# Sliding-window attention and an ELU feed-forward in one kernel: w_in loaded as fp32 and cast on chip, v loaded and shifted by key block, part of ELU on ACT

## The chip, the cores and the metric

The kernel runs on one core of one Trainium2 chip. The metric is device time in microseconds (us). Engines are named as in the profile: PE (TensorE), DVE (VectorE), ACT (ScalarE), POOL (GpSimd), SP (SyncE). Transfers are issued by SP, ACT and POOL, each into its own queue of the same 16 DMA engines: q1 is SP's, q10 ACT's, q0 POOL's.

## The reference

q, k and v have shape 8 x 8 x 576 x 64 (batch, heads, sequence, head size), w_in is 512 x 2048, w_out is 2048 x 512, all fp32.

```python
scores = scale * np.matmul(q, k.transpose(0, 1, 3, 2))        # scale = 1/8
mask = np.abs(pos[:, None] - pos[None, :]) <= 32
scores = np.where(mask, scores, -1e9)
attn = softmax(scores)
x = (attn @ v).transpose(0, 2, 1, 3).reshape(4608, 512)
h = x @ w_in
g = np.where(h > 0.0, h, np.exp(np.minimum(h, 0.0)) - 1.0)
out = g @ w_out
```

## The kernel before

**Attention.** A batch has nine query blocks of 64 rows; two blocks that follow each other make a pair i, and there are 36 pairs. q and k are loaded as fp32 in halves of four heads (`L`, into `stg`), cast to bf16 (`C`, into `bf`), transposed on PE (`T`) and evicted from PSUM (`E`, into `qT` and `kT`). For a pair, `QK` makes the scores of 64 queries against a window of 128 keys, `SM` takes exp on ACT, `MK` multiplies by the band's mask on DVE, `AV` multiplies by v for four heads at a time (g = 0 and 1), with a column of ones that gives the row sum, and `RN` divides. `X` brings the 128 x 512 result into the layout that the feed-forward needs: pairs 0 to 3 over PE and PSUM (`XT`, then a copy `XE`), the others by a DMA transpose from SP.

**v by key block.** `vw` holds v of a batch as nine windows of 128 keys that overlap by half. The even windows are loaded from memory (`LV`, five transfers from POOL that cast to bf16 on the way). The odd windows are made of halves of their even neighbours by two copies from SBUF to SBUF (`SV`, on SP). There are three `vw` buffers.

**Feed-forward.** Tokens go in tiles of 2, 2, then eight times 4 pairs. For each of the 16 column blocks fo of w_in, `H` computes h in PSUM, `EX` takes exp on ACT, `FF` makes f = min(exp(h) - 1, 0) and `GG` makes g = max(h, f), both on DVE. `Y` multiplies by w_out in four parts of four fo each; `YC` evicts and `OUT` stores. w_in and w_out are loaded and cast by POOL's transfers, four each (`WI`, `WO`). `g` has two buffers and `psH`, the PSUM tiles of h, three.

**Order.** Nothing is scheduled by the engines. `Plan` takes every step with an engine, an assumed duration, a rank and its predecessors, replays them in a list schedule, and emits each engine's instructions in the order that comes out. An engine then executes strictly in that order. A step with `at` is assumed to be done no sooner than that; a step with `dma` goes through an assumed transfer server. These assumed times only set the order. The order of the transfers of batches 0 and 1 and of the weights is thereby set on each of SP, ACT and POOL.

The ELU steps in the kernel before:

```python
nc.vector.tensor_scalar(f, e, -1.0, 0.0, ALU.add, ALU.min)      # FF
nc.vector.tensor_tensor(gs[t][:, fo, :], ps, f, ALU.max)        # GG
```

Of the kernel before, what the change touches and what calls it, by code (L numbers as in the profile page):

```python
# [8 lines left out]
FP32 = mybir.dt.float32  # L9
BF16 = mybir.dt.bfloat16  # L10
AX = mybir.ActivationFunctionType
ALU = mybir.AluOpType
# [8 lines left out]
class Plan:  # L21
# [15 lines left out]
    def run(self):  # L37
        ops = self.ops
        done, users, left = {}, {}, {}
        for n, o in ops.items():  # L40
            left[n] = len(o[3])
            for d in o[3]:
                assert d in ops, (n, d)
                users.setdefault(d, []).append(n)
        free = {}
        server = 2.0
        ready = {}
        for n, o in ops.items():
            free.setdefault(o[0], 0.0)
            if left[n] == 0:  # L50
                ready.setdefault(o[0], {})[n] = 0.0
        order = []
        while len(order) < len(ops):
            best = None
            for e, rs in ready.items():
                if not rs:
                    continue
                t = max(free[e], min(rs.values()))
                n = min((ops[n][2], n) for n, r in rs.items() if r <= t)[1]
                if best is None or t < best[0]:  # L60
                    best = (t, e, n)
            t, e, n = best
            del ready[e][n]
            _, dur, _, _, fn, dma, lag, at = ops[n]
            free[e] = t + dur
            if dma:
                server = max(server, t + dur) + dma
                end = server + 2.0
# [20 lines left out]
def kernel(  # L89
# [9 lines left out]
    nc = tc.nc  # L99

    B, H, S, D = q.shape
    WIN = 32
# [4 lines left out]
    QB = 64  # L107
    NQB = S // QB
# [86 lines left out]
            nc.vector.tensor_copy(dst, src)  # L195


    def load_v(b):
        vt = vw[b % NVB]
        vb = v[b].rearrange("h s d -> s h d")  # L200
        nc.gpsimd.dma_start(out=vt[WIN:128, 0, :, 0:D], in_=vb[0:128 - WIN])
        for qb in range(2, NQB - 1, 2):
            lo = qb * QB - WIN
            nc.gpsimd.dma_start(out=vt[:, qb, :, 0:D], in_=vb[lo:lo + 128])  # L204
        lo = (NQB - 1) * QB - WIN
        nc.gpsimd.dma_start(out=vt[0:S - lo, NQB - 1, :, 0:D], in_=vb[lo:S])  # L206

    def shift_v(b):
        vt = vw[b % NVB]
        nc.sync.dma_start(out=vt[0:QB, 1:NQB:2], in_=vt[QB:128, 0:NQB - 1:2])  # L210
        nc.sync.dma_start(out=vt[QB:128, 1:NQB:2], in_=vt[0:QB, 2:NQB:2])


    def QK(i):
# [73 lines left out]

    def XE(i):
        dst, pt = live.pop(("XT", i))  # L290
        nc.vector.tensor_copy(dst, pt)


    gs, es, ys = {}, {}, {}
# [12 lines left out]
    def EX(t, fo):  # L307
# [2 lines left out]
        nc.scalar.activation(e, ps, AX.Exp)  # L310
        es[t, fo] = (ps, e)

    def FF(t, fo):
        ps, e = es[t, fo]
        f = ep.tile([128, ps.shape[1]], BF16, name="f", tag="f")
        nc.vector.tensor_scalar(f, e, -1.0, 0.0, ALU.add, ALU.min)  # L316
        es[t, fo] = (ps, f)

    def GG(t, fo):
        ps, f = es.pop((t, fo))  # L320
        nc.vector.tensor_tensor(gs[t][:, fo, :], ps, f, ALU.max)  # L321

    def ypool(t, c):
        if t < NT - 1:
# [54 lines left out]
    def prank(i):  # L379
# [6 lines left out]
    LAND = {(0, "k", 0): 6.2, (0, "q", 0): 8.2, (0, "k", 1): 10.5,  # L386
            (0, "q", 1): 13.0, (1, "k", 0): 27.0, (1, "q", 0): 31.0,
            (1, "k", 1): 35.0, (1, "q", 1): 39.0}
    for b in range(B):
        need = prank(b * NQB // 2)  # L390
        r0 = need - 60
        t0 = where[b * NQB // 2][0]
        early = [("H", max(t0 - 2, 0), 15 if t0 == 2 else 8)] if b > 1 else []
        for half in range(2):
            for nm in ("q", "k"):
                deps = list(early)
                if b == 1:
                    deps.append(("SM", 0))
                if b:
                    deps.append(("C", b - 1, nm, half))  # L400
                P.op(("L", b, nm, half), "ACT" if b else "SP", 0.1,
                     r0 + half, deps,
                     lambda b=b, nm=nm, half=half: load_qk(
                         b, nm, half, nc.scalar if b else nc.sync),
                     dma=0.0 if b < 2 else 2.2, lag=2.0,
                     at=LAND.get((b, nm, half), 0.0))
                eng = casts0[nm, half] if b == 0 else "POOL"
                deps = [("L", b, nm, half)]
                if b >= 2:
                    deps += [("T", b - 2, nm, hp) for hp in range(HP)]  # L410
                P.op(("C", b, nm, half), eng, cdur[eng], need - 30 + half, deps,
                     lambda b=b, nm=nm, half=half, eng=eng:
                     cast(b, nm, half, engs[eng]))
        deps = list(early)
        if b > 1:
            deps += [("WO", c) for c in range(NWC)]
        if b >= NVB:
            last = ((b - NVB + 1) * NQB - 1) // 2
# [3 lines left out]
        P.op(("LV", b), "POOL", 4.5, (-2000, -899)[b] if b < 2 else r0, deps, lambda b=b: load_v(b),  # L422
             dma=5.0 if b > 1 else 0.0, at=(17.0, 45.0)[b] if b < 2 else 0.0)
        P.op(("SV", b), "SP", 0.2, need - 20, [("LV", b)],
             lambda b=b: shift_v(b), lag=4.5)
        for hp in range(HP):
            for nm in ("q", "k"):
                n = hp * 2 + (nm == "k")
                deps = [("C", b, nm, hp // 2)]
                m = n - (4 if b == 0 else 1)  # L430
                if m >= 0:
                    deps.append(("E", b, "qk"[m % 2], m // 2))
                elif b:
                    deps.append(("E", b - 1, "k", HP - 1))
                P.op(("T", b, nm, hp), "PE", 0.3, need - 36 + 4 * n, deps,
                     lambda b=b, nm=nm, hp=hp: T(b, nm, hp))
                deps = [("T", b, nm, hp)]
                if b >= NKB:
                    last = ((b - NKB + 1) * NQB - 1) // 2
                    deps.append(("QK", last))  # L440
                P.op(("E", b, nm, hp), EVAC[nm, hp], 0.7, need - 36 + 4 * n, deps,
                     lambda b=b, nm=nm, hp=hp: E(b, nm, hp))

    for c in range(NWC):
        P.op(("WI", c), "POOL", 1.0, -990 + c,
             [("C", 0, "k", 1)], lambda c=c: WI(c),
             at=(19.5, 24.0, 28.5, 33.0)[c])
        P.op(("WO", c), "POOL", 1.0, -890 + c, [("C", 1, "q", 1)],
             lambda c=c: WO(c),
             at=(50.0, 54.0, 58.0, 62.0)[c])  # L450

    for i in range(NPAIR):
        r = prank(i)
# [13 lines left out]
        P.op(("MK", i), "DVE", 0.85, r, deps, lambda i=i: MK(i))  # L467
        t, c = where[i]
        for g in range(2):
            deps = [("MK", i)] + [("SV", b) for b in bs]  # L470
            if i < NC0:
                if i:
                    deps.append(("RN", i - 1, g))
# [14 lines left out]
        if i < NC0:  # L488
            if i:
                deps.append(("X", i - 1))  # L490
            P.op(("XT", i), "PE", 0.3, r + 3, deps, lambda i=i: X(i))
            P.op(("X", i), "DVE", 0.42, r + 3, [("XT", i)],
                 lambda i=i: XE(i))
        else:
            P.op(("X", i), "SP", 1.2, r + 3, deps, lambda i=i: X(i), lag=4.0)

    hseq = [(t, fo) for t in range(NT) for fo in range(NFO)]
    for n, (t, fo) in enumerate(hseq):
        np_ = tiles[t][1]
        fr = np_ / 4  # L500
        r = PER * tiles[t][0] + 2 * fo * fr
        deps = [("X", tiles[t][0] + np_ - 1), ("WI", fo * NWC // NFO)]
        if n >= 3:
            deps.append(("GG",) + hseq[n - 3])
        if t >= 2:
# [8 lines left out]
        P.op(("FF", t, fo), "DVE", 0.1 + 0.33 * fr, r, [("EX", t, fo)],  # L514
             lambda t=t, fo=fo: FF(t, fo))
        P.op(("GG", t, fo), "DVE", 0.16 + 0.53 * fr, r, [("FF", t, fo)],
             lambda t=t, fo=fo: GG(t, fo))
# [83 lines left out]
```

The softmax here doesn't subtract the row's maximum and nothing guards it: scores larger than these inputs give would overflow.

## Time and profile before

| what | value |
|---|---|
| median of 3 runs | 367.59 us (363.65 to 368.04) |
| the profiled execution | 366.73 us, its span 364.8 us |
| PE busy | 314.2 us (86%) |
| DVE busy | 252.9 us (69%) |
| ACT busy | 177.2 us (49%) |
| POOL busy | 86.1 us (24%) |
| transfers | 46.13 MB, mean 126 GB/s |

The page gives busy time of each engine, its share in 40 equal slices, the DMA queues, a chain of work followed back from the last instruction, groups of instructions by source line, and transfer issues. Times in the trace's answers are counted from the start of the span. A group's line names the source line, the engine, the operation and the tiles written and read. Matmul ends are modelled, so a busy PE need not be at its peak. The idle time of an engine is named after what ended it.

### The profile page before, as it was taken

The page shows a single profiled execution, that of the slowest core. Times are in us where ns is not written, and L with a number is a line of the kernel's source. Part 1 is how long each engine was busy: PE and PEld are TensorE (multiplying, and loading weights), DVE is VectorE, ACT ScalarE, POOL GpSimd, SP SyncE. Part 2 cuts the span into 40 slices and gives each one's busy share as a digit, 9 for nine tenths or more (in the row PEclk, how much of TensorE's full clock was granted, in tenths as well). Part 3 has the DMA queues.
Part 4 walks back from the last instruction along what each step waited for, and adds up shares of the span by engine and source line. Part 5 has one row for each costly group of instructions (what it writes and reads, how often), then busy time and mean ns, then how long its engine had stood idle before and what let it go on. Part 6 is the DMA issues. An engine that isn't in the chain of part 4 may idle for free.

```text
span 364.8 us, 7010 instructions
## 1 busy us (share of the span) xinstructions
PE 314.2 (86%) x2725; PEld 168.9 (46%) x2768; DVE 252.9 (69%) x565; ACT 177.2 (49%) x290; POOL 86.1 (24%) x93
## 2 busy tenths in 40 slices
PE   1415889669877999999999999989999999999995
PEld 1314666334434544554455445445554444444442
DVE  4216899475779499886887787778788778756610
ACT  3431477236453654754565466555654535443421
POOL 7623810490036004500540240033000000000000
PEclk9999999899999899999999999999999999999999
DMA  8999999999698639994995793195112121111012
GB/s 173 172 251 276 121 198 194 196 135 174 147 242 102 72 101 214 131 138 105 242 127 69 175 210 85 45 234 114 45 51 66 46 58 45 43 49 40 29 65 78
DMA packets 81504, 46.13 MB, mean 126 GB/s; under 512 B 56384, under 2 KB 76864, under 8 KB 81472
## 3 DMA queue, kind: packets, MB, share of 16 engines
q0 software_dynamic: 41728, 8.92, 33.4%
q1 hardware_dynamic: 28544, 20.26, 25.4%
q10 hardware_dynamic: 11200, 16.52, 19.0%
q8 instruction: 21, 0.34, 0.4%
q14 instruction: 11, 0.09, 0.1%
HBM read 36.70 MB, written 9.44 MB: 126 GB/s over the span
## 4 chain that ended last, share of the span: by engine, by line
PE 58%; DVE 18%; DMA 14%; issue 3%; ACTq 2%; POOL 2%; ACT 1%; SPq 1%; POOLq 0%; DVEq 0%
PE psY L335 24%; PE psH L302 24%; DMA vw<-vw 6%; DVE g L321 6%; DVE f L316 6%; DMA xt<-xs 5%; DVE pm L243 4%; PE psO L255 4%; DMA vw<-in_v_dram 3%; PE psT L180 2%; DVE xs L270 2%; ACTq L155 2%; PE psS L220 2%; PE psO L335 1%; PE psS L335 1%
## 5 line engine op out<-in xcount | busy, mean ns | idle before, releaser
L302 PE MATMUL psH<-xt,w_in_sb 128*128 128x512 bf16 (+1 forms) x624 | 147.3, 360 | 4.5 <-DVE g L321 2.4
L310 ACT ACTIVATE e<-psH 128x512 f32<-128x512 f32 (+1 forms) x160 | 88.1, 555 | 115.9 <-PE psH L302 90.1
L335 PE MATMUL psY<-w_out_sb,g 128*128 128x512 bf16 x501 | 131.8, 383 | 3.1 <-ACT y L341 1.1
L316 DVE TENSOR_SCALAR f<-e 128x512 bf16<-128x512 f32 (+1 forms) x160 | 75.7, 473 | 45.8 <-ACT e L310 45.7
L321 DVE TENSOR_TENSOR g<-psH,f 128x512 bf16<-128x512 f32 (+1 forms) x160 | 102.0, 637 | 5.1
L302 PEld LDWEIGHTS <-w_in_sb 128*128 128x128 bf16 x640 | 60.4, 99 | 61.2 <-issue 6.1
L335 PEld LDWEIGHTS <-g 128*128 128x128 bf16 x576 | 52.3, 98 | 55.0 <-issue 2.7
L170 POOL CAST bf<-stg 96x1536 bf16<-96x1536 f32 x29 | 43.5, 1501 | 107.1 <-DMA stg<-in_k_dram 89.1
L255 PE MATMUL psO<-vw,pm 128*128 128x65 bf16 x544 | 30.7, 198 | 17.9 <-DMA vw<-vw 8.3
L231 ACT ACTIVATE pu<-psS 128x1024 bf16<-128x1024 f32 x36 | 36.8, 1021 | 12.7 <-PE psS L220 10.3
L255 PEld LDWEIGHTS <-pm 128*128 128x128 bf16 x576 | 27.1, 102 | 30.9 <-issue 8.1
L243 DVE TENSOR_TENSOR pm<-pu,masks 128x512 bf16<-128x512 bf16 x72 | 34.0, 514 | 4.8 <-ACT pu L231 4.8
L180 PEld LDWEIGHTS <-bf 96*128 96x128 bf16 x384 | 23.7, 104 | 28.2 <-ACT bf L168 8.1
L270 DVE TENSOR_TENSOR xs<-psO,rc 128x256 bf16<-128x256 f32 x68 | 28.9, 424 | 5.5 <-DMA xt<-xs 3.2
L180 PE MATMUL psT<-ident,bf 96*128 96x96 bf16 x348 | 25.4, 211 | 7.0 <-POOL bf L170 3.6
L341 ACT COPY y<-psY 128x512 f32<-128x512 f32 x33 | 19.4, 586 | 19.4 <-PE psY L335 14.3
L268 DVE RECIPROCAL rc<-psO 128x4 f32<-128x4 f32 x68 | 12.1, 178 | 22.0 <-PE psO L255 21.5
L193 ACT COPY qT<-psT 128x576 bf16<-128x576 bf16 x30 | 19.1, 638 | 15.9 <-PE psT L180 15.9
L204 POOL DMA_DIRECT2D vw<-in_v_dram x24 | 21.3, 900 | 15.5 <-PE psO L255 15.3
L220 PE MATMUL psS<-qT,kT 64*128 64x64 bf16 x576 | 16.0, 196 | 3.6 <-ACT pu L231 3.2
L220 PEld LDWEIGHTS <-kT 64*128 64x128 bf16 x576 | 11.3, 98 | 15.3 <-issue 14.5
L206 POOL DMA_DIRECT2D vw<-in_v_dram x8 | 6.5, 812 | 41.4 <-PE psO L255 40.6
(42 smaller groups left out, 74.1 us busy)
## 6 DMA issues: line engine op xcount, KB each, us to landing
out_dram<-y SPq DMA_DIRECT2D x36, 256.0 KB, 2.1
stg<-in_k_dram ACTq DMA_DIRECT2D x14, 576.0 KB, 9.3
stg<-in_q_dram ACTq DMA_DIRECT2D x14, 576.0 KB, 10.9
vw<-vw SPq DMA_DIRECT2D x16, 260.0 KB, 8.5
vw<-in_v_dram POOLq DMA_DIRECT2D x24, 128.0 KB, 8.2
w_in_sb<-in_moe_w_in_dram POOLq DMA_DIRECT2D x4, 512.0 KB, 13.7
w_out_sb<-in_moe_w_out_dram POOLq DMA_DIRECT2D x4, 512.0 KB, 11.3
vw<-in_v_dram POOLq DMA_DIRECT2D x16, 96.0 KB, 11.4
```

What stands on the lines that cost most here:

```text
L170: eng.tensor_copy(dst, src)
L180: nc.tensor.transpose(pt[:, j, :], src[:, j, 2 * hp:2 * hp + 2, :], ident[0:PR, 0:PR])
L220: nc.tensor.matmul(psS[:, h % 2, s, hp, :], lhsT=kT[b % NKB][base:base + 64, hp, qb * QB:qb * QB + 128], rhs=qT[b % NKB][base:base + 64, h ...
L231: nc.scalar.activation(pu, live.pop(("S", i)), AX.Exp, scale=SCALE)
L243: nc.vector.tensor_mul(dst, pu[:, :, s], mb)
L255: nc.tensor.matmul(o[:, j, :], lhsT=p[:, h, s * QB:s * QB + 128], rhs=vw[b % NVB][:, qb, h, :], start=(s == 0), stop=(s == 1))
L270: nc.vector.tensor_mul(live["X", i][:, g * HP:(g + 1) * HP, :], o[:, :, 0:D], rb)
L302: nc.tensor.matmul(ps, lhsT=w_in_sb[:, do, fo * 128:(fo + 1) * 128], rhs=xts[t][:, do, :], start=(do == 0), stop=(do == NDO - 1))
L310: nc.scalar.activation(e, ps, AX.Exp)
L316: nc.vector.tensor_scalar(f, e, -1.0, 0.0, ALU.add, ALU.min)
L321: nc.vector.tensor_tensor(gs[t][:, fo, :], ps, f, ALU.max)
L335: nc.tensor.matmul(ps, lhsT=gs[t][:, fo, c * 128:(c + 1) * 128], rhs=w_out_sb[:, fo, :], start=(fo == 0), stop=(fo == NFO - 1))
```

## The change

- w_in: four transfers `WL` on SP bring it as fp32 into buffers of the `g` pool. Eight casts `WI` (four chunks, two halves each) on POOL and ACT write `w_in_sb`.
- v: `LV` is a step for each even window, and `SV` for batches 0 and 1 is split in two, the first odd window and the other three. `AV` names as its predecessors only the windows that it reads.
- ELU: in tiles 0 and 1, for odd fo, f' = relu(1 - exp(h)) is made on ACT, and g = max(-f', h) on DVE.
- The copy `XE` of pairs 0 to 3 is on ACT.
- The predecessors, ranks and assumed landing times of the loads of batches 0 to 2 and of w_out are changed with it, and with them the order of the instructions.

```diff
-    def load_v(b):
+    def load_v(b, qb):
         vt = vw[b % NVB]
         vb = v[b].rearrange("h s d -> s h d")
...
+        lo, hi = max(0, qb * QB - WIN), min(S, qb * QB - WIN + 128)
+        r = lo - (qb * QB - WIN)
+        nc.gpsimd.dma_start(out=vt[r:r + hi - lo, qb, :, 0:D], in_=vb[lo:hi])
+
+    def shift_v(b, w0, w1):
         vt = vw[b % NVB]
...
+        nc.sync.dma_start(out=vt[0:QB, w0:w1 - 1:2],
+                          in_=vt[QB:128, w0 - 1:w1 - 1:2])
+        nc.sync.dma_start(out=vt[QB:128, w0:w1 - 1:2],
+                          in_=vt[0:QB, w0 + 1:w1:2])
...
     def XE(i):
         dst, pt = live.pop(("XT", i))
-        nc.vector.tensor_copy(dst, pt)
+        nc.scalar.copy(dst, pt)
...
+    def fact(t, fo):
+        return t < 2 and fo % 2 == 1
...
+        if fact(t, fo):
+            nc.scalar.activation(f, e, AX.Relu, bias=1.0, scale=-1.0)
+        else:
+            nc.vector.tensor_scalar(f, e, -1.0, 0.0, ALU.add, ALU.min)
...
+        if fact(t, fo):
+            nc.vector.scalar_tensor_tensor(gs[t][:, fo, :], f, -1.0, ps,
+                                           ALU.mult, ALU.max)
+        else:
+            nc.vector.tensor_tensor(gs[t][:, fo, :], ps, f, ALU.max)
...
-    def WI(c):
-        nc.gpsimd.dma_start(out=w_in_sb[:, :, c * FC:(c + 1) * FC],
-                            in_=w_in_v[:, :, c * FC:(c + 1) * FC])
+    wst = {}
+
+    def WL(c):
+        n = c // 2
+        if n not in wst:
+            wst[n] = gp.tile([128, 2, NDO, FC], FP32, name="g", tag="g")
+        nc.sync.dma_start(out=wst[n][:, c % 2],
+                          in_=w_in_v[:, :, c * FC:(c + 1) * FC])
+
+    def WI(c, half):
+        src = wst[c // 2][:, c % 2, 2 * half:2 * half + 2, :]
+        dst = w_in_sb[:, 2 * half:2 * half + 2, c * FC:(c + 1) * FC]
+        if WENG[half] == "ACT":
+            nc.scalar.copy(dst, src)
+        else:
+            engs[WENG[half]].tensor_copy(dst, src)
...
+    WENG = ("POOL", "ACT")
...
-        early = [("H", max(t0 - 2, 0), 15 if t0 == 2 else 8)] if b > 1 else []
+        early = [("H", max(t0 - 2, 0), 2 if b == 2 else 8)] if b > 1 else []
...
                 if b == 1:
-                    deps.append(("SM", 0))
+                    deps.append(("WI", 1, 1))
...
         if b == 1:
-            deps.append(("C", 0, "k", 1))
...
+            deps.append(("WI", 2, 0))
+        for qb in range(0, NQB, 2):
+            P.op(("LV", b, qb), "POOL", 0.9,
...
+        groups = [(1, 3), (3, 9)] if b < 2 else [(1, 9)]
+        for w0, w1 in groups:
+            P.op(("SV", b, w0), "SP", 1.2, need - 20 + 0.1 * w0,
+                 [("LV", b, x) for x in range(w0 - 1, w1, 2)],
+                 lambda b=b, w0=w0, w1=w1: shift_v(b, w0, w1), lag=4.5)
...
+        P.op(("WL", c), "SP", 0.5, -990 + c, [("L", 0, "q", 1)],
+             lambda c=c: WL(c), at=(16.0, 20.0, 24.0, 28.0)[c])
...
-        P.op(("WO", c), "POOL", 1.0, -890 + c, [("C", 1, "q", 1)],
+        P.op(("WO", c), "POOL", 1.0, -890 + c, [("WI", NWC - 1, 0)],
...
+                if qb % 2 == 0:
+                    deps.append(("LV", b, qb))
+                else:
+                    deps += [("SV", b, w0) for w0, w1 in SVOF[b]
+                             if w0 <= qb < w1]
```

More of the change, by code (lines that the diff above doesn't have):

```diff
@@ L67, in run @@
                 server = max(server, t + dur) + dma
-                end = server + 2.0
+                end = server + 2.0 + lag
             else:
@@ L195, in E @@
             nc.vector.tensor_copy(dst, src)
-    def load_v(b):
+    def load_v(b, qb):
         vt = vw[b % NVB]
         vb = v[b].rearrange("h s d -> s h d")
[L201 to L208, printed above, removed]
+        lo, hi = max(0, qb * QB - WIN), min(S, qb * QB - WIN + 128)
+        r = lo - (qb * QB - WIN)
+        nc.gpsimd.dma_start(out=vt[r:r + hi - lo, qb, :, 0:D], in_=vb[lo:hi])
+    def shift_v(b, w0, w1):
         vt = vw[b % NVB]
-        nc.sync.dma_start(out=vt[0:QB, 1:NQB:2], in_=vt[QB:128, 0:NQB - 1:2])
-        nc.sync.dma_start(out=vt[QB:128, 1:NQB:2], in_=vt[0:QB, 2:NQB:2])
+        nc.sync.dma_start(out=vt[0:QB, w0:w1 - 1:2],
+                          in_=vt[QB:128, w0 - 1:w1 - 1:2])
+        nc.sync.dma_start(out=vt[QB:128, w0:w1 - 1:2],
+                          in_=vt[0:QB, w0 + 1:w1:2])
     def QK(i):
@@ L315, in FF @@
         f = ep.tile([128, ps.shape[1]], BF16, name="f", tag="f")
-        nc.vector.tensor_scalar(f, e, -1.0, 0.0, ALU.add, ALU.min)
+        if fact(t, fo):
+            nc.scalar.activation(f, e, AX.Relu, bias=1.0, scale=-1.0)
+        else:
+            nc.vector.tensor_scalar(f, e, -1.0, 0.0, ALU.add, ALU.min)
         es[t, fo] = (ps, f)
@@ L320, in GG @@
         ps, f = es.pop((t, fo))
-        nc.vector.tensor_tensor(gs[t][:, fo, :], ps, f, ALU.max)
+        if fact(t, fo):
[3 more added lines that the diff above has]
+            nc.vector.tensor_tensor(gs[t][:, fo, :], ps, f, ALU.max)
     def ypool(t, c):
@@ L385 @@
     cdur = {"DVE": 1.2, "ACT": 1.5, "POOL": 1.5}
-    LAND = {(0, "k", 0): 6.2, (0, "q", 0): 8.2, (0, "k", 1): 10.5,
-            (0, "q", 1): 13.0, (1, "k", 0): 27.0, (1, "q", 0): 31.0,
-            (1, "k", 1): 35.0, (1, "q", 1): 39.0}
+    LAND = {(0, "k", 0): 6.2, (0, "q", 0): 7.7, (0, "k", 1): 9.2,
+            (0, "q", 1): 11.0, (1, "k", 0): 30.0, (1, "q", 0): 33.0,
+            (1, "k", 1): 36.0, (1, "q", 1): 39.0}
+    SVOF = {}
+    WENG = ("POOL", "ACT")
     for b in range(B):
@@ L404 @@
                          b, nm, half, nc.scalar if b else nc.sync),
-                     dma=0.0 if b < 2 else 2.2, lag=2.0,
+                     dma=0.0 if b < 2 else 2.2,
+                     lag=2.0 if b < 2 else 5.0,
                      at=LAND.get((b, nm, half), 0.0))
@@ L420 @@
         if b == 1:
-            deps.append(("C", 0, "k", 1))
[L422 to L425, printed above, removed]
+            deps.append(("WI", 2, 0))
+        for qb in range(0, NQB, 2):
+            P.op(("LV", b, qb), "POOL", 0.9,
+                 (-999, -899)[b] + 0.1 * qb if b < 2 else r0 + 0.1 * qb,
+                 deps, lambda b=b, qb=qb: load_v(b, qb),
+                 dma=1.0 if b > 1 else 0.0, lag=2.0,
+                 at=(13.0, 41.0)[b] + 0.6 * qb if b < 2 else 0.0)
+        groups = [(1, 3), (3, 9)] if b < 2 else [(1, 9)]
[3 more added lines that the diff above has]
+                 lambda b=b, w0=w0, w1=w1: shift_v(b, w0, w1), lag=4.5)
+        SVOF[b] = groups
         for hp in range(HP):
@@ L444 @@
     for c in range(NWC):
-        P.op(("WI", c), "POOL", 1.0, -990 + c,
-             [("C", 0, "k", 1)], lambda c=c: WI(c),
-             at=(19.5, 24.0, 28.5, 33.0)[c])
-        P.op(("WO", c), "POOL", 1.0, -890 + c, [("C", 1, "q", 1)],
+        P.op(("WL", c), "SP", 0.5, -990 + c, [("L", 0, "q", 1)],
+             lambda c=c: WL(c), at=(16.0, 20.0, 24.0, 28.0)[c])
+        for half in range(2):
+            P.op(("WI", c, half), WENG[half],
+                 {"ACT": 0.95, "POOL": 1.05, "DVE": 0.7}[WENG[half]],
+                 -980 + c, [("WL", c)],
+                 lambda c=c, half=half: WI(c, half))
+        P.op(("WO", c), "POOL", 1.0, -890 + c, [("WI", NWC - 1, 0)],
              lambda c=c: WO(c),
-             at=(50.0, 54.0, 58.0, 62.0)[c])
+             at=(46.0, 50.0, 54.0, 58.0)[c])
     for i in range(NPAIR):
@@ L469 @@
         for g in range(2):
-            deps = [("MK", i)] + [("SV", b) for b in bs]
+            deps = [("MK", i)]
+            for x in (2 * i, 2 * i + 1):
+                b, qb = divmod(x, NQB)
+                if qb % 2 == 0:
[3 more added lines that the diff above has]
+                             if w0 <= qb < w1]
             if i < NC0:
@@ L491 @@
             P.op(("XT", i), "PE", 0.3, r + 3, deps, lambda i=i: X(i))
-            P.op(("X", i), "DVE", 0.42, r + 3, [("XT", i)],
+            P.op(("X", i), "ACT", 0.42, r + 3, [("XT", i)],
                  lambda i=i: XE(i))
@@ L501 @@
         r = PER * tiles[t][0] + 2 * fo * fr
-        deps = [("X", tiles[t][0] + np_ - 1), ("WI", fo * NWC // NFO)]
+        deps = [("X", tiles[t][0] + np_ - 1), ("WI", fo * NWC // NFO, 0),
+            ("WI", fo * NWC // NFO, 1)]
         if n >= 3:
@@ L513 @@
              lambda t=t, fo=fo: EX(t, fo))
-        P.op(("FF", t, fo), "DVE", 0.1 + 0.33 * fr, r, [("EX", t, fo)],
+        P.op(("FF", t, fo), "ACT" if fact(t, fo) else "DVE",
+             0.1 + 0.33 * fr, r, [("EX", t, fo)],
              lambda t=t, fo=fo: FF(t, fo))
```

## The prediction

> **What bounds the kernel now.** I read the page's row of slices first, then the chain of waits, then busy time by stretch, and last the DMA queues in windows of 2 us.
>
> ```profile
> span 364.8 us, 7010 instructions
> PE   1415889669877999999999999989999999999995
> DVE  4216899475779499886887787778788778756610
> DMA  8999999999698639994995793195112121111012
> ```
>
> A slice is 9.1 us. From the 14th slice on (120 us) PE stands at nine tenths or more. Before that it idles some 40 us in all, and in the same slices the DMA engines are full. The end is therefore moved by whatever moves the first 90 us.
>
> ```profile
> 36.00:48.00 12.00, 10.26 (x99) 7.67 (x98) 10.51 (x33) 6.50 (x16) 9.27 (x10) 1.00 1.98 122
> 48.00:60.00 12.00, 11.12 (x149) 8.11 (x149) 10.90 (x34) 8.65 (x19) 0.00 (x0) 1.00 1.53 208
> 200.00:250.00 50.00, 47.77 (x412) 24.57 (x418) 39.80 (x83) 27.16 (x44) 12.01 (x9) 1.00 0.74 157
> ```
>
> The columns are the stretch, its length, then PE, weight loads, DVE, ACT and POOL busy. Tiles 0 and 1 (36 to 60 us) have DVE at 21.4 of 24 us; later stretches are PE's.
>
> ```profile
> 7.39 11.70 DMA vw<-in_v_dram
> 19.10 10.88 DMA vw<-vw
> 36.12 1.86 PE psH L302 x8
> 60.58 13.35 DMA xt<-xs
> ```
>
> From the chain (start, length): v of batch 0 loads, then the shift of its blocks (SV.0) lands at 30.0, then AV runs, and the first H matmul starts at 36.1. So the gate of the whole kernel is one SBUF copy of 512 packets that lands late in a full DMA system. Why it is late is in the queues (packets, MB, share of 16 engines), here for 4:6, 10:12, 14:16, 18:20 and 34:36 us:
>
> ```profile
> q1 hardware_dynamic: 290, 0.43, 110.0%
> ...
> q1 hardware_dynamic: 286, 0.43, 102.5%
> q0 software_dynamic: 167, 0.02, 16.5%
> ...
> q0 software_dynamic: 2229, 0.28, 359.4%
> ...
> q0 software_dynamic: 399, 0.40, 123.9%
> ...
> q10 hardware_dynamic: 323, 0.48, 82.0%
> q0 software_dynamic: 330, 0.08, 40.9%
> ```
>
> q1 is SP's queue, q10 ACT's, q0 POOL's. POOL issues v at 3.9, yet q0 moves nothing until about 10.5, while q1 runs at 145 packets per us. Alone, v's small packets run at 1,100 per us; beside a queue with work they get one turn for each turn of the other (323 against 330), whatever their size. The w_in load alone makes 200 packets per us.
>
> **What the Trainium skill says.** "DMA: Bandwidth & Descriptors", section "Queues, rings and completion order", says that each DMA engine takes turns between the queue rows it has work for, and that a ring is consumed in order. The trace agrees: 323 against 330, and the four q/k loads on q1 land one after the other (5.7 to 12.3 us after issue). The same page, "SWDGE vs HWDGE vs iDMA", says that only GpSimd's DMAs can cast, so fp32 loads from SP need casts on engines. "ScalarE: Activation LUTs", section "Table sets: the hidden batching unit", says relu is in every table set, so exp and relu need no switch; the trace has one table load (1.28 us at 0.80), but no relu.
>
> **The change, part by part.**
>
> *w_in on SP (WL).* Four loads of 512 packets of 2 KB now follow the q/k loads on q1 at about 2.8 us, with no wait. On the order of the changed program SP then issues SV.0 behind them, so in q1's ring the shifts cannot start before w_in has passed. q1 has sent 1,181 packets by 10 us and the last of the 1,536 q/k packets passes at about 12.7. For w_in beside v: a 2 KB packet takes 99 ns (123.9% x 32 us / 399) and a v packet about 33; the full windows overlap by a factor 1.2 (82.0 + 40.9%), so a pair costs 110 ns on each of 16 engines, 145 pairs per us. Bounds: 200 per us (w_in alone) and 120 (w_out's pace beside SV.1 at 50 us). I take 145: w_in passes at 12.7 + 14.1 = 26.8 us (22.9 to 29.8).
>
> *v of batch 0.* Turn by turn with q1 it gets only 290 + 2,048 = 2,340 of its 4,608 packets by then; before it had all at 17.1. The first small shift (128 packets) passes by 27.7 and lands at about 29.2. So pair 0 gains a microsecond at most, although its own v blocks are in by 25.
>
> *The loads of batch 1 (L.1).* They now stand on ACT behind WI.1.1: SM.0, the cast WI.0.1 (1.0 us; the 96x1536 cast took 1.47), SM.1, SM.2, WI.1.1 end at about 24.0. Before, 3.5 us passed from issue to first packet, so q10 wakes at 27.5, just when q1 is done. Three of the four loads (1,152 packets at 160 per us, 7.2 us) then hold v to their pace: v has 2,470 + 1,150 at 34.9, the last 990 take 0.9, and v lands at about 37.0. If w_in is as fast as its bound, v is through at 25 and lands at 26; if q10 wakes 2 us later, at 31.
>
> *The second shift (SV.0.3).* It needs the last v block. Two issues of 0.6, 384 packets at 116 per us (SV beside v, 84 to 86 us) 3.3, 0.7 to the first packet, 1.2 to land: 42.8 against 30.0 before. Pair 1 needs it, and H.0.0 needs pair 1. In the changed program the fourth load of L.1 waits for the semaphore that the first half of this shift raises (eight semaphores go round among the SP and ACT transfers). Behind that issue on ACT stand SM.3, XE.0, WI.2.1 and XE.1 (0.8 + 1.0 + 0.4 + 1.0 + 0.4). AV.1, its normalisation and XT.1 take about 2.4 beside them. H.0.0 starts at about 45.3, 9.2 later than at 36.1; QK.3, AV.0 and three w_in casts are then done, which is why the 12.8 shrink.
>
> *Casts of w_in on POOL.* Hidden: they wait for data, and POOL has nothing due. WO now waits on POOL for v to land (again the round of semaphores), and the casts of batch 1 stand behind it until about 48; T.1 is due behind H.0.13, at about 55. Without that cover it would cost what POOL is late.
>
> *f on ACT for half of tiles 0 and 1, XE on ACT.* DVE loses 16 x 0.29 and 4 x 0.42 = 6.3 us and keeps the g instructions: the new one reads the same PSUM operand, so I price it at the old 0.42 (0.40 to 0.55). ACT gains 16 x 0.40 (priced at e's 0.38 plus gap; 0.33 to 0.5). Its sum from EX.0.0 to EX.1.15: e 32 x 0.40 = 12.8, f 6.0, seven q/k evictions 4.6, two SM 2.1, XE 0.9, WI.3.1 1.0, L.2's issues 2.4: 29.8. DVE ran this stage at 92% before, so ACT gets 31 us. PE's work there is only 22.6.
>
> *Order of PE.* AV.4 to AV.8 and almost all of Y.0 and Y.1 move out of tile 1's H stage to a stretch of their own before H.2.0: 10 AV x 0.41, 8 T x 0.42, 4 QK x 0.41, 11 Y x 0.86 = 18.6, with hand-overs 20. L.2 is issued earlier relative to the compute, so the PE stall for its cast (66.4 to 69.5 before) goes.
>
> *Sum.* With as many H and Y groups behind it as the changed kernel has at H.2.0, the kernel before stood at 89.9 us: 53.8 after its H.0.0. Now it is 31 + 20 = 51. Total: +9.2 - 2.8 = +6.4. The same PE work is left from there on, and steady tiles are untouched. The profiled execution took 366.7 (span 364.8 and 1.9 around it), 0.9 below the median shown, so 366.7 + 6.4 = 373.1; I say 373.
>
> **The rivals.** A is the forecast: v is held to the pace of w_in and then of L.1. For it: the equal turns at 34 to 36 us. Its own range, from w_in's pace and q10's start, is 367 to 379.
>
> B: the gate opens when w_in is through. If v is in before q10 wakes, SV.0.3 follows w_in directly and lands at 30 to 31; with the shorter way to H this gives H.0.0 at 34, and 366.7 - 2 - 2.8 = 362; if DVE's relief gives the whole 4.5 us that f was worth and PE's T stall (3.1) goes too, 357. For it: w_in alone ran at 200 per us. Against: w_in is not alone, and v starts at 10.5 only.
>
> C, the slower side: ACT as the bound of tiles 0 and 1. Place: EX, f and the evictions in one in-order queue, where an eviction of batch 1 waits for PE's T and everything behind it waits too. 29.8 us of work at 80% instead of 96% is 37 us, +6 on the forecast: 379. It decides from about 33 us on, where the total passes 375. For it: ACT waited 90 us in all for H before and its f now joins that loop. Against: f waits on its own engine's e, which saves one hand-over.
>
> **How the numbers follow.** A 0.48, B 0.20, C 0.32. Two per cent, 7.3 us, is about what a measurement of this kernel can tell from no change: under 360.2 and over 375. A gives 0.32 within and 0.16 slower, B 0.11 faster and 0.09 within, C 0.05 within and 0.27 slower: faster 0.11, same 0.46, slower 0.43. The range 361 to 382 leaves out B's best and C's worst.
>
> **What would show it.** Right: q0 and q1 with equal counts from 11 to 27 us; v's last packets at 35 or later; the first AV near 29 and the second a dozen microseconds after it; H.0.0 at 43 to 47; ACT over nine tenths in the two slices after. Wrong: H.0.0 before 38, q0 at over 300 packets per us beside w_in, or steady tiles that differ.

## The result, and the profile after

The changed kernel takes 380.1 us (median of 4 runs, 378.8 to 382.1) against 367.6 before: ratio 1.036, 95% interval 1.028 to 1.044, slower. Forecast were 373.0 us and a range of 361 to 382. The profiled execution took 378.8 us, with a span of 377.1 (364.8 before). The ratios in this document leave disturbed executions out, so a median shown beside one can lie higher than the ratio says.

The page's rows of slices, after (a slice is 9.4 us):

```profile
span 377.1 us, 7071 instructions
PE   1502387899697799999899989998999999999995
DVE  5211275874389777978897688669868887756510
ACT  4430377874354356465456446554765544444321
DMA  8999993999979819995997294349111221101011
```

PE has a longer hole in slices 3 to 5 (19 to 47 us: 0, 2, 3), and the DMA engines have one in their seventh slice (57 to 66 us: 3). The chain of waits up to 50 us (start, length):

```profile
7.42 27.22 DMA vw<-in_v_dram
34.66 8.78 DMA vw<-vw
46.50 1.01 PE psH L301 x4
```

The last v load of batch 0 is in the chain for 27.2 us (11.7 before), the shift of its later blocks begins at 34.7 (19.1), and H.0.0 stands at 46.5 (36.1). The queues at 14:16, 24:26 and 34:36 us (packets, MB, share of 16 engines) say why:

```profile
q1 hardware_dynamic: 319, 0.63, 93.0%
q0 software_dynamic: 316, 0.04, 29.5%
...
q1 hardware_dynamic: 246, 0.50, 73.5%
q0 software_dynamic: 244, 0.03, 23.6%
q10 hardware_dynamic: 101, 0.16, 20.5%
...
q0 software_dynamic: 1087, 0.14, 237.1%
q10 hardware_dynamic: 106, 0.16, 45.1%
```

v (q0) gets one packet for each packet of w_in (q1), 316 for 319. From 24.9 us on batch 1's q and k (q10) take turns too. q10 is empty between 31.7 and 34.9, and there q0 goes on at about 1,000 packets per us. ACT's line of time adds another long wait:

```profile
29.98 0.32 ACTq L155 DMA_DIRECT2D stg<-in_k_dram  x1
42.42 0.32 ACTq L155 DMA_DIRECT2D stg<-in_q_dram  x1
42.87 1.02 ACT L230 ACTIVATE pu<-psS 128x1024 bf16<-128x1024 f32 x1 [20.12 <-POOL bf L170]
```

Of the four loads of batch 1 the third is issued at 30.0 and the fourth at 42.4 (all four at 18.2 to 19.9 before); the softmax behind them waits 20.1 us. The bracket names POOL's cast, which is long done. The fourth issue follows the landing of the first half of the second shift at 42.35, and the third that of the first shift at 29.96: each raises the semaphore that the load takes next.

The stretches (us; then PE, weight loads, DVE, ACT and POOL busy):

```profile
46.50:60.00 13.50, 11.90 (x103) 9.09 (x103) 9.69 (x29) 10.54 (x28) 1.47 (x1) 1.00 0.83 169
60.00:75.00 15.00, 12.03 (x135) 8.79 (x135) 10.98 (x23) 11.83 (x30) 7.06 (x7) 1.00 0.80 165
200.00:250.00 50.00, 48.37 (x432) 25.11 (x430) 38.46 (x80) 28.16 (x45) 7.80 (x6) 1.00 0.55 108
```

Tiles 0 and 1 now have DVE at 72% and ACT at 78%: no engine is full.

To compare kernels whose PE orders differ, I add up PE's matmuls in the order of their weight loads, each at its undisturbed duration (0.216 us for 128x512), and ask when each kernel has done the same sum. Times in us; the columns a2, b1, c3 and b3 are experiments told below.

| work done | before | after | a2 | b1 | c3 | b3 |
|---|---|---|---|---|---|---|
| 10 | 38.9 | 49.3 | 30.7 | 50.7 | 41.7 | 34.4 |
| 20 | 52.1 | 64.3 | 58.5 | 66.8 | 59.0 | 50.3 |
| 50 | 89.9 | 97.2 | 87.6 | 97.4 | 94.2 | 87.7 |
| 60 | 100.7 | 108.5 | 107.6 | 107.0 | 103.6 | 97.5 |
| 110 | 154.4 | 164.5 | 163.1 | 163.7 | 156.4 | 150.7 |
| 250 | 289.0 | 300.7 | 299.8 | 301.1 | 294.1 | 284.3 |

After is 10.4 us late at the start, has regained 3.1 by the start of H.2.0 (97.2), and loses 4.4 more, 2.8 of them by the row for 110. Column a2 is the surprise: it starts 8 us ahead of before and ends as late as the changed kernel.

### The profile page after: what moved, and what is told of

The parts are those of the page before. It is cut to its first block, busy times and chain, and to the rows that moved or that the text cites. A ratio compares the mean times of both kernels' runs of the same rounds, so it can differ in the third digit from the quotient of the medians.

```text
span 377.1 us, 7071 instructions
## 1 busy us (share of the span) xinstructions
PE 317.5 (84%) x2768; PEld 169.4 (45%) x2768; DVE 249.2 (66%) x545; ACT 188.2 (50%) x314; POOL 87.1 (23%) x93
## 4 chain that ended last, share of the span: by engine, by line
PE 61%; DVE 18%; DMA 11%; ACT 3%; ACTq 2%; issue 2%; POOL 2%; SPq 0%; POOLq 0%
PE psH L301 25%; PE psY L344 24%; DMA vw<-in_v_dram 7%; DVE f L321 6%; DVE g L330 5%; PE psO L254 4%; DVE pm L242 3%; PE psT L180 3%; DMA vw<-vw 2%; PE psS L219 2%; ACTq L155 2%; DVE xs L269 2%; ACT e L309 2%; DMA out_dram<-y 1%; PE psS L344 1%
## 5 line engine op out<-in xcount | busy, mean ns | idle before, releaser
L301 PE MATMUL psH<-xt,w_in_sb 128*128 128x512 bf16 (+1 forms) x640 | 149.8, 363 | 9.3 <-DVE g L330 3.3
L344 PE MATMUL psY<-w_out_sb,g 128*128 128x512 bf16 x528 | 134.6, 381 | 1.0 <-ACT y L350 1.0
L321 DVE TENSOR_SCALAR f<-e 128x512 bf16<-128x512 f32 (+1 forms) x144 | 72.2, 502 | 44.0 <-ACT e L309 43.5
L330 DVE TENSOR_TENSOR g<-psH,f 128x512 bf16<-128x512 f32 (+1 forms) x144 | 95.3, 662 | 5.0
L230 ACT ACTIVATE pu<-psS 128x1024 bf16<-128x1024 f32 x36 | 36.8, 1022 | 26.6 <-POOL bf L170 20.1
L254 PEld LDWEIGHTS <-pm 128*128 128x128 bf16 x576 | 27.4, 102 | 45.6 <-DVE pm L242 11.8
L203 POOL DMA_DIRECT2D vw<-in_v_dram x40 | 34.2, 864 | 38.3 <-PE psO L254 38.3
L267 DVE RECIPROCAL rc<-psO 128x4 f32<-128x4 f32 x68 | 12.1, 178 | 34.8 <-PE psO L254 34.4
L193 ACT COPY qT<-psT 128x576 bf16<-128x576 bf16 x30 | 19.1, 636 | 8.8 <-PE psT L180 8.7
L219 PEld LDWEIGHTS <-kT 64*128 64x128 bf16 x576 | 11.3, 98 | 14.2 <-issue 13.3
L193 ACT COPY kT<-psT 128x576 bf16<-128x576 bf16 x21 | 13.4, 638 | 7.7 <-PE psT L180 7.7
```

The lines of the kernel that those rows point to most:

```text
L219: nc.tensor.matmul(psS[:, h % 2, s, hp, :], lhsT=kT[b % NKB][base:base + 64, hp, qb * QB:qb * QB + 128], rhs=qT[b % NKB][base:base + 64, h ...
L230: nc.scalar.activation(pu, live.pop(("S", i)), AX.Exp, scale=SCALE)
L254: nc.tensor.matmul(o[:, j, :], lhsT=p[:, h, s * QB:s * QB + 128], rhs=vw[b % NVB][:, qb, h, :], start=(s == 0), stop=(s == 1))
L301: nc.tensor.matmul(ps, lhsT=w_in_sb[:, do, fo * 128:(fo + 1) * 128], rhs=xts[t][:, do, :], start=(do == 0), stop=(do == NDO - 1))
L344: nc.tensor.matmul(ps, lhsT=gs[t][:, fo, c * 128:(c + 1) * 128], rhs=w_out_sb[:, fo, :], start=(fo == 0), stop=(fo == NFO - 1))
```

## The experiments

### One part alone, or one part undone (a1 to a4)

**a1: f and XE back on DVE.**

```diff
-        nc.scalar.copy(dst, pt)
+        nc.vector.tensor_copy(dst, pt)
...
-        return t < 2 and fo % 2 == 1
+        return False
...
-            P.op(("X", i), "ACT", 0.42, r + 3, [("XT", i)],
+            P.op(("X", i), "DVE", 0.42, r + 3, [("XT", i)],
```

> The changed kernel with f of tiles 0 and 1 and the copy XE back on DVE; w_in, v and their order as changed. Gate theory (w_in's turns in the queues hold v and its shift): H.0.0 stays at 46 to 47 us, and the total moves by no more than what f was worth on ACT, 0 to 4 us: 378 to 384. Rival, ACT as the bound of tiles 0 and 1: the 29 us from the first H to the last of tile 1 shorten, total under 374.

Measured: 376.8 to 384.0 us, ratio to before 1.035 (1.018 to 1.052); H.0.0 at 46.7. f on ACT is neither the cause nor a visible gain here.

**a2: w_in behind both shifts of batch 0.**

```diff
-        P.op(("WL", c), "SP", 0.5, -990 + c, [("L", 0, "q", 1)],
-             lambda c=c: WL(c), at=(16.0, 20.0, 24.0, 28.0)[c])
+        P.op(("WL", c), "SP", 0.5, -990 + c, [("SV", 0, 3)],
+             lambda c=c: WL(c), at=(25.0, 28.5, 32.0, 35.5)[c])
```

> The changed kernel with one predecessor changed: the four w_in loads on SP wait in the order behind both shifts of batch 0 instead of before them. Gate theory: v lands at 18 to 19 as in the kernel before, the second shift lands at 22 to 24, w_in passes in 11 to 14 us after it, H.0.0 starts at 28 to 31 instead of 46.5, and the total falls by most of that: 358 to 368. Rival, the loss is in ACT or in the order of steps behind H.2: total stays above 374.

Measured: 377.4 to 382.8 us, ratio 1.035 (1.024 to 1.046). The start did all that was expected of it, H.0.0 at 27.9 instead of 46.5. The end hardly moved: the medians differ by 1.7 us and the intervals of the two ratios lie over each other. Mending the start alone brings nothing. That does not clear the late start of the changed kernel, because a2 loses its lead in waits that the changed kernel does not have. PE waits 4.1 us, up to 37.2, for a copy of xt that stands on ACT behind the fourth load of batch 1, which goes out at 36.2 when a piece of w_in lands. Then it waits 6.0 us for a g of DVE:

```profile
54.46 3.27 PE L301 MATMUL psH<-xt,w_in_sb 128*128 128x256 bf16 x16 [6.04 <-DVE g L330]
```

The clock adds to it. Up to 130 us PE is busy for 17.6 us while the granted clock stands at one half, in before and after for 6.6 us each. If such work takes twice its time, a2 loses 5 to 6 us more by it; this is an estimate from those busy times.

**a3: before, with f and XE on ACT.** The edit is that part of the change.

> The kernel before with only f (odd fo of tiles 0 and 1) and XE moved to ACT. Gate theory: the start stays (H.0.0 at 35.5 to 36.5) and DVE's relief shortens tiles 0 and 1 by 0 to 5 us: total 362 to 368. Rival, ACT becomes the bound: 370 or more.

Measured: ratio 1.011 (0.9995 to 1.023), median 371.2 us. That lies over the forecast and where the rival put it (370 or more), but the trace has another reason than ACT. Up to 88 us it runs 1.8 us ahead of before, then PE waits 5.3 us for the shift of batch 2:

```profile
PE psO L255 <- DMA vw<-vw: 5.3, 1, 5.3
```

**a4: before, with v's loads and shifts split and nothing else of the change.**

> The kernel before with only the v loads and shifts split by key block; w_in still by POOL's casting loads. Gate theory: the first shift needs only two of five v loads, is issued near 16 and lands near 18 to 20, the second is issued at 18 to 19 as before and lands at 27 to 30 beside w_in and the loads of batch 1: H.0.0 at 33 to 36, total 363 to 368. Rival, the split itself costs (more issues, more waits on SP and POOL): 370 or more.

Measured over 20 runs: ratio 0.993 (0.989 to 0.997), a small gain. In the profiled execution, which took 367.0 us and so more than the median of 365.6, the first AV comes 8.7 us earlier, the work at H.0.0 4.7, and by 102 us all of it is gone, the last of it in the same wait for batch 2's shift (1.9 us at 93.8) and a stretch of half granted clock from 94.1 to 97.5. So neither part alone makes the loss, and what each gains early is taken back in the middle.

### A second gate: v of batch 2 (b1 to b4)

From a2 to a4 I formed the theory of a second gate: the v loads of batches 2 to 4, the shifts and the transposes of pairs 4 to 7 fall together at 75 to 97 us. All four b kernels issue batch 2's v early, since its buffer is free from the start (in b4, where the five loads are one step, with 65.0 as the assumed landing):

```diff
-        if b > 1:
+        if b == 2:
+            deps = [("C", 1, "q", 1)]
+        elif b > 1:
             deps += [("WO", c) for c in range(NWC)]
...
-                 (-999, -899)[b] + 0.1 * qb if b < 2 else r0 + 0.1 * qb,
+                 (-999, -899, -880)[b] + 0.1 * qb if b < 3 else r0 + 0.1 * qb,
...
-                 at=(13.0, 41.0)[b] + 0.6 * qb if b < 2 else 0.0)
+                 at=(13.0, 41.0, 62.0)[b] + 0.6 * qb if b < 3 else 0.0)
```

> The changed kernel with one edit: the v loads of batch 2 are issued on POOL right behind batch 1's casts (about 48 us) and not behind batch 2's casts (72 us), so that they fill the hole of the DMA engines at 57-70 us; their buffer is free from the start. Two-gate theory (a second gate of v loads, shifts and transposes at 75-97 us sets when H.2.0 begins, and cost the last 5 us of the 12): SV.2 and X.7 come 4 to 6 us earlier, H.2.0 at 91-94 instead of 97.2, end 373-376 (380 before the edit). Rival, that H.2.0 is late only because the start was late and PE had the same work left: H.2.0 at 96-98 and the end unchanged, 378-382.

b1 (after + this): 376.4 to 379.5 us, ratio 1.027 (1.020 to 1.034). The second chain line of each pair here is H.2.0, the first what it waited for; after, then b1:

```profile
91.91 5.32 DMA out_dram<-y
97.23 4.42 PE psH L301 x12
```

```profile
90.84 6.41 DMA xt<-xs
97.39 2.75 PE psH L301 x12
```

The store named for after is not what H.2.0 reads: the last transpose of its x lands at 97.1, in b1 at 97.2. H.2.0 doesn't come earlier, against the forecast, but PE now waits 1.2 us for it instead of 2.9, and its first 12 matmuls run at full speed (2.75 us) instead of taking 4.4 at a granted clock of 0.88 over 90 to 100 us. From work 50 to 60 b1 needs 9.6 us, after 11.3. The intervals of the two ratios overlap, and at work 250 b1 stands at 301.1 and after at 300.7. What a second gate is worth is not settled.

> Both gates opened: w_in behind batch 0's shift on SP (H.0.0 was at 27.9 there), and v of batch 2 issued right behind batch 1's casts. Two-gate theory: H.2.0 at 89-93 instead of 98, end 367-373 (378 with the first gate alone). If the work between 30 and 58 us (ACT waiting for late pieces of w_in, late q and k loads of batch 1) is what ate the 8 us of the start and not the second gate: H.2.0 stays at 96-98 and the end at 376-379.

b2 (a2 + this): 378.3 to 383.9 us, ratio 1.036 (1.027 to 1.046). A clear miss: by the ratio some 381 us, 8 over the forecast and over its rival's 376 to 379 too. Opening both gates brings nothing.

> The kernel before with the v loads split by key block (365.6, H.0.0 earlier than before) and v of batch 2 issued right behind w_out on POOL. Two-gate theory: the wait of 1.95 us for SV.2 at 93.8 goes and the 2 to 4.7 us won at the start come through: 360-364, the best of all so far. Rival, that the v loads of batch 2 were not late in that kernel, which issued batch 3's first: within 1.5 us of 365.6.

b3 (a4 + this): ratio 0.989 (0.980 to 0.999), which is 364 us and within the forecast; the wait for batch 2's shift is gone from the trace and the lead of the start stays (3.2 us at work 60, 4.7 at 250). By its interval it can't be told from a4 (0.993).

> The kernel before with only v of batch 2 issued right behind w_out on POOL. In the kernel before nothing waited for the second gate at 90-97 us for long, since its start was 5 to 8 us later than with the split loads. Two-gate theory: 365-368, at most 2 us under before's 367.6. Rival, that these loads set the middle of every variant: 362-364.

b4 (before + this): ratio 1.000 (0.998 to 1.002), as forecast. Issuing v of batch 2 early brings nothing to the kernel before, and with w_in on the fp32 route nothing that the times show (b1, b2); beside the split loads it takes a wait away.

### Batch 1's q and k (c1, d1, c3), and a best version (c2)

**c1: a2 with b's edit, and with q and k of batch 1 issued behind the first softmax and cast on POOL ahead of w_out's issues.** The assumed landing times of w_in, of w_out and of batch 1's q and k change with it.

```diff
-                    deps.append(("WI", 1, 1))
+                    deps.append(("SM", 0))
...
-        P.op(("WO", c), "POOL", 1.0, -890 + c, [("WI", NWC - 1, 0)],
+        P.op(("WO", c), "POOL", 1.0, -890 + c, [("C", 1, "q", 1)],
```

> Still w_in as fp32 through the g buffers on SP, cast on POOL and ACT, v split, f of the leading tiles on ACT: but w_in's loads stand behind both shifts of batch 0, the q and k loads of batch 1 are issued on ACT behind the first softmax (as in the kernel before) and not behind a cast of w_in, POOL casts batch 1's q and k ahead of w_out's issues, and v of batch 2 is issued behind w_out. If the changed kernel's loss is a matter of order alone (the start, batch 1's q and k late, batch 2's v late): H.0.0 at 28-31, no wait of PE over 3 us between 30 and 60 us (with the start alone mended there were 6.0 and 4.1), H.2.0 at 88-92, end 362-368. Rival, that the fp32 route itself costs (its pieces arrive too slowly behind the shifts for H.0, and the casts hold ACT): PE waits 6 us or more between 28 and 60 again, end 373-378.

Measured: ratio 1.035 (1.026 to 1.043), another miss, and it looked like the rival's win. H.0.0 came at 36.4, not at 28 to 31, and the trace shows that the edit had not done what it said. POOL, which was to cast batch 1's q and k as they land, stood in its queue behind w_in's pieces and cast the last three at 47.9 to 52.3. That showed what after, a2 and c1 have in common. The first scores of batch 1 (QK.4) start on PE at, in order, before, after and a2:

```profile
53.98 0.70 PE L220 MATMUL psS<-qT,kT 64*128 64x64 bf16 x16
```

```profile
71.64 0.41 PE L219 MATMUL psS<-qT,kT 64*128 64x64 bf16 x16
```

```profile
70.70 0.41 PE L219 MATMUL psS<-qT,kT 64*128 64x64 bf16 x16
```

In c1 it is 71.4. H.0.0 differs by 18 us among the three slow ones and QK.4 by one. The other three slow kernels have it at 70.8 (a1), 72.4 (b2) and 74.0 (b1). Their last cast of batch 1 ends at 52.9 (after), 53.8 (a2) and 52.3 (c1), against 40.8 before. In a2 the four casts then run in one piece, and take DVE with them:

```profile
48.10 5.69 POOL L170 CAST bf<-stg 96x1536 bf16<-96x1536 f32 x4
```

```profile
47.69 6.26 DVE L321 TENSOR_SCALAR f<-e 128x256 bf16<-128x256 f32 x1
```

An f that takes 0.28 us elsewhere takes 6.26 and ends with the last cast (POOL's line of time, then DVE's). PE's wait of 6.0 us in a2 ends behind this f.

**d1: before, with batch 1's q and k late and nothing else.**

```diff
-            (0, "q", 1): 13.0, (1, "k", 0): 27.0, (1, "q", 0): 31.0,
-            (1, "k", 1): 35.0, (1, "q", 1): 39.0}
+            (0, "q", 1): 13.0, (1, "k", 0): 36.0, (1, "q", 0): 39.0,
+            (1, "k", 1): 42.0, (1, "q", 1): 45.0}
...
-                    deps.append(("SM", 0))
+                    deps.append(("H", 0, 0))
```

> The kernel before with one edit: the q and k loads of batch 1 are issued on ACT behind the first hidden matmul of tile 0 and not behind the first softmax (18 us), so that batch 1's last cast ends about 52 us as in the changed kernel (52.9; 40.8 before), while v, its shift, w_in and the start of H.0.0 (36 us) stay as they are. New theory, that batch 1's q and k and not the start set the middle: QK.4 begins at 66-71 instead of 54.0 (71.6 in the changed kernel, 70.7 with its start mended), the transposes of pairs 4 to 7 and three batches of v fall together at 78-96, H.2.0 at 95-99, end 373-379. Rival, that the changed kernel's time came from its late start: H.0.0 and the end as before, 366-369.

Measured: 373.4 us median, ratio 1.013 (1.005 to 1.021). That is the lower end of what the theory gave (373 to 379), and 4.7 us by the ratio (1.7 to 7.7 by its interval). The profiled execution took 381.7 us, 8 more than the median, so I take only the order from it: the work at H.0.0 is in time (36.5 us at work 10, 38.9 before), H.2.0 at 96.5 as forecast, and QK.4 at 62.2, ahead of the 66 to 71 forecast. The edit also tells the planner of later loads, so T.1, QK.4 and the pairs behind them move behind more of tile 1's H in PE's order, as in the changed kernel. Late data and late order weren't tried apart.

**c3: the fp32 route, with batch 1's q and k early.**

```diff
-    WENG = ("POOL", "ACT")
+    WENG = ("DVE", "ACT")
...
-                    deps.append(("WI", 1, 1))
+                    deps.append(("SM", 3 if (nm, half) == ("q", 1) else 0))
...
-            deps.append(("WI", 2, 0))
+            deps.append(("C", 1, "k", 0))
...
-        P.op(("GG", t, fo), "DVE", 0.16 + 0.53 * fr, r, [("FF", t, fo)],
+        P.op(("GG", t, fo), "DVE", 0.16 + 0.53 * fr, r, [("FF", t, fo)]
+             + [("WI", 2 * t + 1, x) for x in range(2) if t < 2],
```

The rest of its edit is c1's, with landings of 24 to 36 us assumed for batch 1's q and k and 29 to 41 for w_in.

> The fp32 route with batch 1's q and k as early as before: w_in's loads behind both shifts of batch 0; q and k of batch 1 on ACT behind the first softmax, the fourth behind the fourth softmax so that its issue holds nothing; w_in's casts on DVE and ACT, so that POOL casts batch 1's q and k as they land; v of batch 2 behind w_out. The two g buffers hold w_in until its casts are through, so the first tile's g waits for half of w_in (39-42 us). New theory: batch 1's last cast at 38-44, QK.4 at 54-60, H.2.0 at 90-94, end 364-371, near before and 10 us under the changed kernel although H.0 is held to 39 us. Rival, that the fp32 route costs by itself: 375 or more.

Measured: 372.1 to 374.0 us, ratio 1.016 (1.009 to 1.022). It lies between the two forecasts, and its interval does not meet the changed kernel's: 6.8 us of the 12.5 come back in the medians, while w_in still takes the fp32 route. The edit changes several things at once, so the gain can't be given to one of them. H.0.0 stands at 41.1 there, 13 us later than in a2, and the kernel is faster than a2 all the same, with a mean granted clock of 0.991 (a2 0.962).

```profile
57.20 0.65 PE L219 MATMUL psS<-qT,kT 64*128 64x64 bf16 x16
```

QK.4 is back at 57.2, within the forecast. The last cast of batch 1 comes at 47.5 (38 to 44 was said) and H.2.0 at 86.9 (90 to 94). What remains has names in the waits of PE from 20 to 112 us and in ACT's line of time:

```profile
PE psT L284 <- ACT xt L290: 8.2, 1, 8.2
PE psO L254 <- DMA vw<-vw: 4.2, 1, 4.2
```

```profile
36.12 0.33 ACTq L155 DMA_DIRECT2D stg<-in_q_dram  x1
36.49 0.58 ACT L290 COPY xt<-psT 128x512 bf16<-128x512 bf16 x1 [13.16 <-DMA g<-in_moe_w_in_dram]
```

The fourth load of batch 1 is again held on ACT, now until a piece of w_in lands at 36.0, and the copy of xt behind it stands 13.2 us. A version without that wait was not tried.

**c2: b3, with f and XE on ACT as well.**

> The kernel before with the v split, batch 2's v behind w_out, and f of the leading tiles and the copy of xt on ACT; w_in stays with the casting DMA. In the kernel before, f on ACT alone gained 1.8 us up to 88 us and lost it at the wait for SV.2 near 100. With batch 2's v early, two-gate theory: 1 to 2 us under the same kernel with f on DVE (363.6 over its undisturbed runs), 361-363. Rival, f on ACT moves the order so that another wait takes it: 363-368.

Measured: ratio 0.986 (0.979 to 0.994), which is 362.5 us and within the forecast, the lowest ratio of all, with single runs at 359.5 and 359.6 us. It can't be told from b3 (0.989). Both are ahead of the kernel before, by about a per cent, and of the changed one, and both leave w_in on the casting transfer.

## Why the prediction was right, and where its reason was not

The forecast was 7 us low and the measured time lies in the range. That is in part luck: the forecast's own mechanism, A, reached only to 379, and 380.1 is covered because rival C stretched the range to 382, by a mechanism that did not show. The likeliest of the three outcomes given was no change. Step by step:

**Equal turns: right. The time at which w_in has passed: right by two errors.** q0 and q1 stay level from 11 to 26.5 us. The pace of w_in beside v was taken as 145 pairs per us and was 160 (319 and 316 in 2 us), and q10 woke at 24.9 instead of 27.5 and took turns with w_in's last part (in 1 us from 25 on each queue moves 97). The last packet of w_in starts at 27.4 (26.8 was said).

**v, the shift, H.0.0: right in the sum, with errors that cancel.** v landed at 34.6 and not at 37.0, since only two loads of batch 1 stood beside it: the third waited for the first shift to land, while the prediction names such a wait for the fourth alone. The second shift then took 8.8 us from there and not 5.8, beside the third load and v of batch 1. (With both issues of 0.6 us counted, as the prediction lists them, its own sum is 6.4 us and ends at 43.4.) The shift landed at 43.4 (42.8), the first AV went on at 30.1 and the second at 43.5, H.0.0 began at 46.5 (45.3): +10.4 for +9.2.

**The stage of tiles 0 and 1: right in size, wrong in kind.** 29.0 us for 31 from H.0.0 to the last H of tile 1 (75.5), then 21.7 for 20 to H.2.0: 50.7 us for 51. But ACT at over nine tenths, named as what would show it, isn't there: 78%. f on ACT cost 0.42 (0.40 taken) and the new g 0.42, as priced, and with relu beside exp the changed kernel still has one table load (1.28 us). Rival C's total of 379 is near the measured one without its mechanism, since a1 takes f off ACT and stays at 1.035.

**"The same PE work is left from there on, and steady tiles are untouched": the term that failed.** It was put at nothing and measured 4.4 us: +7.3 at H.2.0, +11.7 at work 250. Between work 50 and 60 only 0.5 us of it are lost, although the first 12 matmuls of H.2.0 take 1.7 us more than in b1 at a lower granted clock: before needs 10.8 us for this piece of work, after 11.3 and b1 9.6. Over the same work between 60 and 180 (108.5 to 233.7 us after, 100.7 to 221.6 before) the loss is 4.3 us, and PE waited for masked scores, after and then before:

```profile
PE psO L254 <- DVE pm L242: 6.2, 4, 3.2
```

```profile
PE psO L255 <- DVE pm L243: 2.2, 4, 0.9
```

That is 4.0 us more. Both kernels have one stretch of half granted clock in this work (from 117.1 before, from 124.8 after), so the clock makes no difference there. The longest of these waits, 3.15 us, ends at 124.9, behind two f on DVE of 1.15 and 1.48 us, 1.8 us over their medians, while POOL casts the last two pieces of batch 3 (119.95 to 123.53). "SBUF — State Buffer", section "Who interferes with whom", in the Trainium skill says that a DVE instruction in a two-port mode (tensor_scalar on SBUF operands can enter one), or one with two SBUF inputs, shares a pair of ports with GpSimd by an exclusive lock, and that the second to come blocks fully. The trace agrees: f reads and writes SBUF and is stretched to the end of the cast (1.48 here against a median of 0.43 for 128x512, 6.26 above against 0.28 for 128x256); pm, with two SBUF inputs, took up to 1.72 us (median 0.42); g reads one operand from PSUM and never took over 0.70. But the stretching itself is not new: added up, f and pm take 19 us beyond their medians before and 20 after, and before, batch 3's casts run at 105.4 to 113.7, 9.7 us earlier and so at about the same work. What differs is how long PE waits for the stretched instructions. That the changed order puts AVs behind them is my reading; no run takes that order apart.

**The casts of batch 1: hidden as waits, and still a part of the loss.** The prediction hid them behind H.0.13, with T.1 due at about 55. The last cast ended at 52.9, not at 48, and T.1 came at 57.8, so PE waited for none of these casts. But in this order T.1 stands 16 us later than before; after, then before:

```profile
57.78 0.42 PE L180 MATMUL psT<-ident,bf 96*128 96x96 bf16 x6
```

```profile
41.93 0.42 PE L180 MATMUL psT<-ident,bf 96*128 96x96 bf16 x6
```

Only part of these 16 us is the later start (10.4). What a later place of batch 1 in PE's order costs was not asked in the prediction. d1 puts it at 4.7 us (1.7 to 7.7) in the kernel before, for late data and late order together. c3 gets 6.8 us of the changed kernel's 12.5 back, with other repairs beside it.

**What the 12.5 us are.** The changed kernel's own trace has 10.4 us at the start, 3.1 regained and 4.4 lost later. That the start is mended in a2 without a gain shows that the parts don't add, and not that the start costs nothing. No run splits the 12.5 us among the start, the order of batch 1, the lock on DVE and the clock, and what the fp32 route itself costs stays open.

**Rival B** (the gate opens with w_in) fell as its own test said: H.0.0 wasn't before 38.

## What to carry to other kernels

Two delays that run beside each other don't add: before the first is priced, ask what would be late next if it were gone. An instruction that stands at nearly the same time in all slow versions (here QK.4) is a lead, and becomes a cause only when a run moves it alone. A load that is issued later moves twice in a planned order, once as data and once through the landing time that the planner assumes. And an issue that waits for a semaphore holds its whole engine: the fourth load of batch 1 let ACT's next step wait 20.1 us in the changed kernel, 13.2 in c3 and 5.0 in a2. A cast given to POOL is priced with the DVE instructions that it locks out, best where DVE reads PSUM or idles.

## What the runs showed of the hardware that I had not expected

A DVE instruction on SBUF operands can be held for as long as four POOL casts back to back: 6.26 us for one of 0.28. PE's granted clock fell in several kernels, with the row of the page for a2, whose early H phase has PE waiting again and again, as the plainest case:

```profile
PEclk9999669998599899999999999999999999999999
```

Slices 5 and 6 (38 to 56 us) are at six tenths and slice 11 (94 to 103) at five. The Trainium skill, "TensorE: Matmul & The Clock Gate", section "HAM oscillation — how this bites in real kernels", says that idle gaps of about 3.4 us and more drop the clock. The trace agrees for the long gaps: waits of PE of 4.1 us (up to 37.2) and 6.0 us (up to 54.5) stand ahead of the first of these slices and in the second. The changed kernel waits 11.1 us up to 43.5. Its granted clock is 1.00 from 44 to 50, but its matmuls are slow there all the same, four of H.0.0 against four of the same shape 11 us later:

```profile
46.50 1.01 PE L301 MATMUL psH<-xt,w_in_sb 128*128 128x256 bf16 x4 [0.23 <-ACT xt L290]
57.34 0.60 PE L301 MATMUL psH<-xt,w_in_sb 128*128 128x256 bf16 x4 [0.16 <-DVE g L330]
```

So the row of the granted clock doesn't show every slow stretch. Nor is a gap of that length needed: in the kernel before the granted clock falls to one half at 117.1, and no wait of PE in the nine microseconds ahead of it is over 1.0 us.
